# A fused convolution and gated product: row halves of product 2 that share one tile, a moved half-way mark, and new orders for the first four tiles

## The chip, the cores and the metric

The kernel runs on one core of a Trainium2 chip. The metric is the device time of one execution in microseconds, the median of ten runs. Five engines work side by side, each through its own queue in order: TensorE (PE, with its weight loads shown as PEld), VectorE (DVE), ScalarE (ACT), GpSimd (POOL) and SyncE (SP), which here issues nearly all transfers. Engines wait for one another through semaphores.

## The reference, cut to what matters

The input `x` has 8 sequences of 4096 tokens with 192 channels. The first stage is a causal convolution over seven tokens whose weights, one set for each of 8 heads, are a softmax; a head owns 24 channels. The second stage is two matrix products with a gate between them:

```python
w = softmax(weight)                                  # [8, 7]
c = einsum('hk,bskhg->bshg', w, windows_of_7(x))     # causal, zeros ahead of a sequence
h = c.reshape(32768, 192) @ w_in                     # [32768, 2048]
g = h * cos(h)
out = (g @ w_out).astype(float32)                    # [32768, 192]
```

## The kernel before, in words

**Tiles and units.** The 32768 tokens are cut into 64 tiles of 512 (`T`, `NT`) and, for the convolution, into 32 units of 1024 (`U`, `NU`); a unit serves two tiles. The loop over `t` (L409) runs 66 times: in iteration `t` the kernel makes product 1 and the gate for tile `t`, works on product 2 of earlier tiles, and prepares the convolution of unit `t // 2 + 2`, one half of its heads in the even iteration and the other in the odd one.

**A unit's path.** SP loads the unit and its edges (`load_unit`, `load_edges`, L68 to L76), POOL casts it (`cast_unit`, L175), PE convolves it with band matrices (`conv_part`, L214: steps `c1` and `c2`), ACT takes the result out (`ec1`, `ec2`), POOL doubles each row (`double_unit`, L245), SP issues a DMA transpose into `cT` (`turn_unit`, L249), and POOL mends the first tokens of each block of 128 (`mend_edges`, L257). `x_f`, `x_bf`, `ct` and `cT` have two buffers each.

**Product 1 and the gate.** `mm1` (L339) makes one of eight blocks of a tile, `h0` to `h7`: six matmuls of 64 rows by 512 tokens, in pairs that run side by side in the upper and the lower half of the array. A block takes one of three buffers of PSUM, a ring that the convolution's banks also come from. `gcu` (L351), written `s0` to `s7`, takes the sine on ACT and multiplies on DVE, and frees the buffer.

**Product 2.** A step (`mm2_step`, L364) is a pair of 64-row matmuls. There are two banks, `b` = 0 and 1, each for two of a tile's four blocks of 128 tokens. Both row halves of the array have to be summed into each bank[...]. Before the change the upper half works on bank `b` of phase `p`, and the lower half one phase later on the same bank: 129 phases of 32 steps, of which the first and the last have only one half at work. `evac` (L386) copies a finished bank out on ACT, and `store` (L391) sends a tile to memory from SP's queue.

**The turn.** Where the halves change banks, `Turn` (L159 to L170) puts a no-op into SP's queue: the no-op waits for the last matmuls on PE, and the next matmuls on PE wait for the no-op. The convolution does the same between `c1` and `c2`, except in units 0 to 2. In a trace the no-ops are SPq rows of L164.

**Orders.** What each iteration issues on PE is written out in a string: `h3` is a block of product 1, `m12` twelve steps of product 2, `c1` and `c2` the convolution. A second string has the order on ACT and DVE: `s3` is the gate, `P` and `Q` the evacuations of banks 0 and 1. `PE_FIRST` and `ACT_FIRST` are for the first tiles, where `r` is the convolution of unit 0's second half (`conv_rest`, L318) and `d1`, `d2` a further convolution. `p` and `q` in the PE string are only marks: what they release in the program's order is written below the loop over the string (L457 to L478). Since every queue is in order, a mark's place in the string settles where its transfers stand among SP's other entries and its copies among POOL's:

```python
            if k == "q":
                if second == 0 and t and u + 1 < NU:
                    turn_unit(u + 1)
                    mend_edges(u + 1)
                if t == 1:
                    turn_unit(1)
                    cast_unit(3)
                    mend_edges(1)
                if second == 0 and u + 3 < NU:
                    cast_unit(u + 3)
```

**The start.** Unit 0 is loaded, convolved and turned in two parts. Its first half (`conv_first`, `turn_first`) goes through PE for the transpose; its second half is `r`, whose four copies ACT and DVE share, after which POOL doubles it, SP issues its transpose and the loads of unit 2, and POOL casts `w_out`.

Of the kernel before, what the change touches and what calls it, by code (L numbers as in the profile page):

```python
# [8 lines left out]
FP32 = mybir.dt.float32  # L9
# [7 lines left out]
def kernel(  # L17
# [8 lines left out]
    nc = tc.nc  # L26
# [41 lines left out]
    def load_edges(u, queue=nc.sync):  # L68
        queue.dma_start(out=x_tiles[u][:, UB, :],
                          in_=xf[u * U - 8 : u * U - 8 + U, :].rearrange("(n t) d -> n t d", t=128)[:, 0:16, :])  # L70

    def load_unit(u, n0=0, n1=UB, queue=nc.sync):
        if n0 == 0:
            x_tiles[u] = xin.tile([128, UB + 1, D], FP32, name="x_f")
        queue.dma_start(out=x_tiles[u][:, n0:n1, :],
                          in_=xf[u * U + n0 * 128 : u * U + n1 * 128, :].rearrange("(n p) d -> p n d", p=128))  # L76
# [119 lines left out]
    def conv_out(u, c, ps, n0, m0, m1, copy, double=False, banks=(0, 1)):  # L196

        for b in banks:
            w0 = (2 * c + b) * 2 * R
            o = ct_tiles[u][:, m0:m1, :, :, w0 : w0 + 2 * R].rearrange("p n k t w -> p (n k) t w")  # L200
            i = ps[b][:, (m0 - n0) * 2 * G : (m1 - n0) * 2 * G].rearrange("p (m t w) -> p m t w", t=1, w=2 * R)
            if double:
                copy(o, i.to_broadcast([128, (m1 - m0) * NC, 2, 2 * R]))
            else:
                copy(o[:, :, 0, :], i[:, :, 0, :])  # L205

    def ring_banks():
        h = h_pool.tile([128, 2, T], FP32, name="h")
        return [h[:, 0, :], h[:, 1, :]]
# [35 lines left out]
    def double_unit(u, n0=0, n1=UB + 1):  # L245
        ct = ct_tiles[u]
        nc.gpsimd.tensor_copy(out=ct[:, n0:n1, :, 1, :], in_=ct[:, n0:n1, :, 0, :])  # L247

    def turn_unit(u, n0=0, n1=UB + 1):  # L249
        ct = ct_tiles.pop(u)  # L250
        if u not in cT:
            cT[u] = cT_pool.tile([128, UB + 1, NC, 128], BF16, name="cT")
        nc.sync.dma_start_transpose(out=cT[u][:, n0:n1].rearrange("p n c k -> p (n c) k"),
                                    in_=ct[:, n0:n1].rearrange("p n c t k -> p (n c t k)"))
        cT.pop(u - 2, None)
# [62 lines left out]
    def conv_rest():  # L318
        banks = o_banks()
        for c in range(2):  # L320
            for i in range(4):
                for prev in range(2):
                    conv_mm(0, c, [b[:, 4 * G * 2 * c :] for b in banks], i, slice(0, 128), NB + 1 - prev, UB + 1 - prev, prev,
                            start=c == 0 and prev == 0 and i % 2 == 0, stop=c == 1 and prev == 1 and i % 2 == 1)
        for b in range(2):
            for c in range(2):
                conv_out(0, c, [x[:, 4 * G * 2 * c :] for x in banks], NB, NB, UB, copies[1 - b], banks=(b,))

    conv_first()
    turn_first(0)  # L330
# [31 lines left out]
    STEPS = 2 * NF  # L362

    def mm2_step(q):  # L364
        phase, i = divmod(q, STEPS)
        f, si = divmod(i, 2)
        for r in range(2):
            tt, b = divmod(phase - r, 2)
            if not 0 <= tt < NT:
                continue  # L370
            if r == 0 and i == 0:

                last = (tt, b) == (NT - 1, 1)
                o_ps[tt, b] = ring_banks()[0] if last else o_pools[b].tile([128, T], FP32, name="o_ps%d" % b)
            rows = slice(64 * r, 64 * r + 64)
            s = 2 * b + si
            m = nc.tensor.matmul(out=o_ps[tt, b][:, si * D : (si + 1) * D],  # L377
                                 lhsT=g_tiles[tt][rows, f, s * 128 : (s + 1) * 128], rhs=wo[rows, f // 2, f % 2, :],
                                 start=(r == 0 and i == 0), stop=(r == 1 and i == STEPS - 1), skip_group_check=True)
            if r == 0 and i == STEPS - 1:  # L380
                turns[tt, b] = Turn()
                turns[tt, b].mark(m)
            if r == 1 and i == 0:
                turns.pop((tt, b)).wait(m)

    def evac(t, b):  # L386
        if b == 0:
            o_sb[t] = opool.tile([128, NB, D], FP32, name="o_sb")
        nc.scalar.copy(o_sb[t][:, 2 * b : 2 * b + 2, :].rearrange("p s d -> p (s d)"), o_ps.pop((t, b))[:, 0 : 2 * D])  # L389

    def store(t, b0=0, b1=2):  # L391
        nc.sync.dma_start(out=out[t * T + b0 * 256 : t * T + b1 * 256, :].rearrange("(n p) d -> p n d", p=128),
                          in_=o_sb[t][:, 2 * b0 : 2 * b1, :])

    o_ps, o_sb, turns = {}, {}, {}
# [1 line left out]

    PE_ORDER = "h0 m7 c1 m6 c2 m4 h1 m7 q h2 h3 m12 h4 m10 h5 m10 h6 h7 p m8"  # L400
    ACT_ORDER = "s0 ec1 ec2 s1 Q s2 s3 s4 s5 P s6 s7"

    PE_FIRST = ["h0a h0b h1 r h2 h3 h4 d1 d2 h5 h6 c1 c2 h7 p m12",
                "h0 m8 h1 m12 q h2 h3 h4 m4 d1 d2 m8 h5 m8 h6 c1 c2 m8 h7 m4 p m8"]
    ACT_FIRST = ["s0a s0b s1 s2 s3 s4 ed1 ed2 s5 s6 ec1 ec2 s7", "s0 s1 s2 s3 s4 ed1 ed2 s5 s6 ec1 ec2 P s7"]

    HALVES = {"": (0, NB), "a": (0, NB // 2), "b": (NB // 2, NB)}
    step = 0
    for t in range(NT + 2):  # L409
        u, second = divmod(t, TPU)  # L410
        cu, cc = (u + TPU, second) if t >= TPU else (1 + t, 1)
        conv = {"c": conv_part(cu, cc, ring_banks if t else o_banks, t < TPU) if cu < NU else iter(())}
        if t < TPU:
            conv["d"] = conv_part(cu, 0, ring_banks if t else o_banks, True)
        act, done, h = (ACT_ORDER if t > 1 else ACT_FIRST[t]).split(), set(), {}

        def flush():
            while act:
                k = act[0]
                need = {"P": "p", "Q": "q", "e": k[1:2] + "2"}.get(k[0], "h" + k[1:])  # L420
                if need not in done:
                    return
                act.pop(0)
                if k == "P" and 0 <= t - 1 < NT:
                    evac(t - 1, 0)
                elif k == "Q" and 0 <= t - 2 < NT:
                    evac(t - 2, 1)
                elif k[0] == "e":
                    next(conv[k[1]], None)
                elif k[0] == "s" and t < NT:  # L430
                    gcu(t, int(k[1]), h.pop(k[1:]), *HALVES[k[2:]])

        for k in (PE_ORDER if t > 1 else PE_FIRST[t]).split():
            if k[0] == "h" and t < NT:
                h[k[1:]] = mm1(t, int(k[1]), *HALVES[k[2:]])
            elif k[0] in conv:
                next(conv[k[0]], None)
            elif k == "r":
                conv_rest()
                double_unit(0, NB, UB)  # L440
                turn_unit(0, NB, UB)
                load_unit(2)
                load_edges(2)
                for q in range(2):
                    nc.gpsimd.tensor_copy(out=wo[:, q * HP : (q + 1) * HP], in_=wo_f[:, q * HP : (q + 1) * HP])  # L445
            elif k[0] == "m":
                for q in range(step, step + int(k[1:])):
                    mm2_step(q)
                step += int(k[1:])
            elif k[0] == "p":  # L450
                assert step % (2 * STEPS) == 0
            elif k[0] == "q":
                assert step % (2 * STEPS) == STEPS
            done.add(k)
            flush()
# [8 lines that stand above are left out]
                    mend_edges(1)  # L464
                if second == 0 and u + 3 < NU:
                    cast_unit(u + 3)
                if second == 1 and t > 1 and cu < NU:
                    double_unit(cu)
                if t == NT + 1:
                    store(NT - 1, 1, 2)  # L470
            if k == "p":
                if t < NT + 1 and 0 <= t - 2:
                    store(t - 2)
                if t == NT:
                    store(NT - 1, 0, 1)
                if second == 1 and u + 4 < NU:
                    load_unit(u + 4)
                    load_edges(u + 4)  # L478
        if t == 0:
            double_unit(1)  # L480
            load_unit(3)
            load_edges(3)
            cast_unit(2)
        if t == 1:
            double_unit(2)
# [30 lines left out]
```

## Time and profile before

| what | value |
|---|---|
| median of 10 runs | 720.44 us (720.24 to 721.1) |
| the profiled execution | 720.35 us |
| its span, first to last instruction | 718.6 us |
| granted TensorE clock, mean | 0.999 |
| PE busy | 708.1 us (99%) |
| PE weight loads busy | 530.3 us (74%) |
| ACT busy | 617.7 us (86%) |
| DVE busy | 611.4 us (85%) |
| POOL busy | 149.7 us (21%) |
| start of h0 of tiles 1, 2 and 63 | 22.04, 35.48 and 695.98 us |
| DMA transposes on SP's queue | 32, median 4.11 us each |

Times in the timeline count from the first instruction. A row of PE gives the start of its first matmul and the end of its last, so that rows overlap a little; the start of the next row tells when PE was free again. A row on SP's queue (SPq) is the time that the issue of a transfer took there, not the transfer itself. The chain of waits is followed back from the last instruction, and shows which engine's work set the end. Each group of instructions has its busy time, the mean length of one, and the idle time ahead of it with what ended it.

### The profile page before, as it was taken

The page shows a single profiled execution, that of the slowest core. Times are in us where ns is not written, and L with a number is a line of the kernel's source. Part 1 is how long each engine was busy: PE and PEld are TensorE (multiplying, and loading weights), DVE is VectorE, ACT ScalarE, POOL GpSimd, SP SyncE. Part 2 cuts the span into 40 slices and gives each one's busy share as a digit, 9 for nine tenths or more (in the row PEclk, how much of TensorE's full clock was granted, in tenths as well). Part 3 has the DMA queues.
Part 4 walks back from the last instruction along what each step waited for, and adds up shares of the span by engine and source line. Part 5 has one row for each costly group of instructions (what it writes and reads, how often), then busy time and mean ns, then how long its engine had stood idle before and what let it go on. Part 6 is the DMA issues. An engine that isn't in the chain of part 4 may idle for free.

```text
span 718.6 us, 26315 instructions
## 1 busy us (share of the span) xinstructions
PE 708.1 (99%) x11826; PEld 530.3 (74%) x11827; DVE 611.4 (85%) x536; ACT 617.7 (86%) x781; POOL 149.7 (21%) x124
## 2 busy tenths in 40 slices
PE   7899999999999999999999999999999999999997
PEld 3577777777777777777777777777777777777776
DVE  6788888888888888888888888888888888888984
ACT  7888888888888898888888888888888888888884
POOL 5621122221122221022220222220122221121000
PEclk9999999999999999999999999999999999999999
DMA  8745544455534356534455434566434455324312
GB/s 217 181 122 144 137 101 121 86 136 145 125 108 115 88 144 145 113 108 115 100 145 145 117 101 104 114 144 145 109 109 96 123 145 143 103 67 89 80 46 67
DMA packets 183664, 85.24 MB, mean 119 GB/s; under 512 B 111616, under 2 KB 183168, under 8 KB 183552
## 3 DMA queue, kind: packets, MB, share of 16 engines
q1 hardware_dynamic: 183128, 82.78, 46.9%
q8 instruction: 92, 1.51, 0.9%
q0 software_dynamic: 416, 0.79, 0.7%
q14 instruction: 20, 0.16, 0.1%
q10 hardware_dynamic: 8, 0.00, 0.0%
HBM read 31.36 MB, written 25.17 MB: 79 GB/s over the span
## 4 chain that ended last, share of the span: by engine, by line
PE 95%; DMA 2%; POOL 1%; ACT 1%; DVE 0%; issue 0%; SPq 0%; DVEq 0%; POOLq 0%
PE o_ps L377 46%; PE h L347 45%; PE h L190 3%; DMA wo_f<-in_moe_w_out_dram 1%; DMA x_f<-in_x_dram 1%; PE h L377 0%; POOL x_bf L179 0%; POOL wo L445 0%; ACT L148 0%; PE o_ps L292 0%; DVE g L358 0%; DVEq L511 0%; ACT x_bf L179 0%; ACT cs L354 0%; POOL mask L128 0%
## 5 line engine op out<-in xcount | busy, mean ns | idle before, releaser
L358 DVE TENSOR_TENSOR g<-h,cs 128x1024 bf16<-128x1024 f32 (+1 forms) x513 | 603.6, 1218 | 93.8 <-ACT cs L354 89.0
L354 ACT ACTIVATE cs<-h 128x1024 bf16<-128x1024 f32 (+1 forms) x513 | 511.3, 1026 | 59.3 <-PE h L347 52.2
L377 PEld LDWEIGHTS <-g 64*128 64x128 bf16 x8192 | 362.2, 94 | 85.9 <-SPq L164 1.2
L377 PE MATMUL o_ps<-wo,g 64*128 64x192 bf16 x8128 | 423.9, 243 | 1.7 <-ACT o_sb L389 0.6
L347 PE MATMUL h<-cT,w 64*128 64x512 bf16 (+1 forms) x3078 | 398.5, 376 | 0.3 <-DVE cT L316 0.2
L347 PEld LDWEIGHTS <-w 64*128 64x128 bf16 x3078 | 154.7, 94 | 85.3 <-issue 1.1
L259 POOL COPY cT<-cT 128x144 bf16<-128x144 bf16 x31 | 9.5, 307 | 496.1 <-DMA cT<-ct 325.2
L179 POOL CAST x_bf<-x_f 128x1728 bf16<-128x1728 f32 (+1 forms) x32 | 80.5, 2515 | 9.0 <-DMA x_f<-in_x_dram 8.9
L205 ACT CAST ct<-h 128x432 bf16<-128x432 f32 x120 | 56.4, 522 | 27.4 <-PE h L190 26.9
L389 ACT COPY o_sb<-o_ps 128x384 f32<-128x384 f32 x127 | 60.1, 473 | 4.9 <-PE o_ps L377 4.9
L247 POOL COPY ct<-ct 128x1728 bf16<-128x1728 bf16 (+1 forms) x32 | 51.3, 1602 | 18.5 <-ACT ct L205 18.3
L190 PE MATMUL h<-x_bf,band 64*128 64x216 bf16 (+1 forms) x472 | 42.7, 254 | 1.0 <-POOL x_bf L179 1.0
L190 PEld LDWEIGHTS <-band 64*128 64x128 bf16 (+1 forms) x496 | 22.2, 94 | 7.0 <-issue 4.4
L105 PE MATMUL o_ps<-zero 128*128 128x512 bf16 x12 | 5.5, 630 | 1.3 <-DVE zero L100 1.3
L377 PE MATMUL h<-wo,g 64*128 64x192 bf16 x64 | 5.8, 243 | 0.0
L105 PEld LDWEIGHTS <-zero 128*128 128x128 bf16 x15 | 1.7, 129 | 3.5 <-issue 2.2
L190 PE MATMUL o_ps<-x_bf,band 128*128 128x96 bf16 (+1 forms) x24 | 1.9, 223 | 2.4 <-POOL x_bf L179 2.4
L205 ACT CAST ct<-o_ps 128x432 bf16<-128x432 f32 (+1 forms) x6 | 2.4, 461 | 1.0 <-PE o_ps L190 0.9
L445 POOL CAST wo<-wo_f 128x1536 bf16<-128x1536 f32 x2 | 2.9, 1464 | 0.8 <-DMA wo_f<-in_moe_w_out_dram 0.8
L389 ACT COPY o_sb<-h 128x384 f32<-128x384 f32 x1 | 0.5, 478 | 2.4 <-PE h L377 2.4
L115 ACT ACT_TABLE_LOAD x1 | 1.3, 1283 | 1.4 <-PEq L500 1.4
L292 PEld LDWEIGHTS <-band 128*128 128x128 bf16 x32 | 1.1, 96 | 1.2 <-POOL band L279 1.2
(47 smaller groups left out, 27.2 us busy)
## 6 DMA issues: line engine op xcount, KB each, us to landing
out_dram<-o_sb SPq DMA_DIRECT2D x63, 384.0 KB
x_f<-in_x_dram SPq DMA_DIRECT2D x31, 768.0 KB
x_f<-in_x_dram SPq DMA_DIRECT2D x31, 96.0 KB
wo_f<-in_moe_w_out_dram SPq DMA_DIRECT2D x4, 384.0 KB
x_f<-in_x_dram SPq DMA_DIRECT2D x2, 384.0 KB
w<-in_moe_w_in_dram POOLq DMA_DIRECT2D x2, 384.0 KB, 6.3
cT<-ct SPq DMA_TRANSPOSE x32
out_dram<-o_sb SPq DMA_DIRECT2D x2, 192.0 KB
```

The source lines that it names most:

```text
L105: nc.tensor.matmul(out=bank, lhsT=zero[:, 0:128], rhs=zero, start=True, stop=True)
L179: copy(out=bf[u][:, n0 + o : n1 + o, :].rearrange("p n (h k r) -> p (n h) k r", k=NC, r=R), in_=x_tiles[u][:, n0:n1, :].rearrange("p n (h ...
L190: return nc.tensor.matmul(out=ps[i // 2][:, 0 : (n1 - n0) * 2 * G].rearrange("p (n k i r) -> p i n k r", n=n1 - n0, k=NC, i=2)[:, i % 2], ...
L205: copy(o[:, :, 0, :], i[:, :, 0, :])
L247: nc.gpsimd.tensor_copy(out=ct[:, n0:n1, :, 1, :], in_=ct[:, n0:n1, :, 0, :])
L259: nc.gpsimd.tensor_copy(out=cT[u][:, 0:UB, :, 0 : K - 1], in_=cT[u][:, UB].rearrange("p c (n t) -> p n c t", t=16)[:, :, :, 8 : 8 + K - 1])
L347: nc.tensor.matmul(out=h[:, i, n0 * 128 : n1 * 128], lhsT=w[rows, k, j, :], rhs=c[rows, m0 + n0 : m0 + n1, k, :], start=(k == 0), stop=(k ...
L354: nc.scalar.activation(out=cs[:, :, part], in_=h[:, :, part], func=AF.Sin, bias=math.pi / 2.0, scale=1.0)
L358: nc.vector.tensor_tensor(out=g_tiles[t][:, 2 * j : 2 * j + 2, part], in0=h[:, :, part], in1=cs[:, :, part], op=ALU.mult)
L377: m = nc.tensor.matmul(out=o_ps[tt, b][:, si * D : (si + 1) * D], lhsT=g_tiles[tt][rows, f, s * 128 : (s + 1) * 128], rhs=wo[rows, f // 2, ...
L389: nc.scalar.copy(o_sb[t][:, 2 * b : 2 * b + 2, :].rearrange("p s d -> p (s d)"), o_ps.pop((t, b))[:, 0 : 2 * D])
L445: nc.gpsimd.tensor_copy(out=wo[:, q * HP : (q + 1) * HP], in_=wo_f[:, q * HP : (q + 1) * HP])
```

## The change

*Product 2.* A tile now has 64 steps in one run. In its first 32 the upper row half sums bank 0 and the lower one bank 1; in the other 32 they have changed places. One turn for each tile, in its middle, holds both matmuls of a pair. Both banks of a tile are finished together.

*Evacuation and stores.* Both banks are evacuated behind the mark `p`: bank 0 by ACT, bank 1 by DVE. The last tile has both banks in the ring, and its two halves are stored from SP's and from ACT's queue.

*Marks.* `p` now stands where a tile is finished, behind `h2`, and `q` where it is half done, behind `h6`; before they stood at the end of the string and behind `h1`. The doubling of a unit, the store of a tile and the loads go with `p` (the loads of iteration 1 with `q`); the transpose, the mending and the cast stay with `q`.

*The start.* Four tiles have orders of their own. `r` comes two blocks later. Its copies become an entry `er` of the ACT order, write each row twice, and POOL's doubling of that half goes; the transpose, the loads of unit 2 and the casts of `w_out` are issued with `er`.

```diff
@@ conv_rest
+        yield
         for b in range(2):
             for c in range(2):
-                conv_out(0, c, [x[:, 4 * G * 2 * c :] for x in banks], NB, NB, UB, copies[1 - b], banks=(b,))
+                conv_out(0, c, [x[:, 4 * G * 2 * c :] for x in banks], NB, NB, UB, copies[1 - b], True, (b,))
+        yield
@@ mm2_step
-        phase, i = divmod(q, STEPS)
-        f, si = divmod(i, 2)
+        tt, i = divmod(q, 2 * STEPS)
+        half, k = divmod(i, STEPS)
+        f, si = divmod(k, 2)
...
         for r in range(2):
-            tt, b = divmod(phase - r, 2)
...
+            b = half ^ r
             rows = slice(64 * r, 64 * r + 64)
             s = 2 * b + si
...
+        if i == STEPS - 1:
+            turns[tt] = Turn()
+            turns[tt].mark(*ms)
+        if i == STEPS:
+            turns.pop(tt).wait(*ms)
@@ evac, store
-        nc.scalar.copy(o_sb[t][:, 2 * b : 2 * b + 2, :].rearrange("p s d -> p (s d)"), o_ps.pop((t, b))[:, 0 : 2 * D])
+        copies[b](o_sb[t][:, 2 * b : 2 * b + 2, :].rearrange("p s d -> p (s d)"), o_ps.pop((t, b))[:, 0 : 2 * D])
...
@@ orders
-    PE_ORDER = "h0 m7 c1 m6 c2 m4 h1 m7 q h2 h3 m12 h4 m10 h5 m10 h6 h7 p m8"
-    ACT_ORDER = "s0 ec1 ec2 s1 Q s2 s3 s4 s5 P s6 s7"
+    PE_ORDER = "h0 m1 c1 m6 c2 m4 h1 m10 h2 p h3 m10 h4 m9 h5 m9 h6 m4 q h7 m11"
+    ACT_ORDER = "s0 ec1 ec2 Q s1 P s2 s3 s4 s5 s6 s7"
-    PE_FIRST = ["h0a h0b h1 r h2 h3 h4 d1 d2 h5 h6 c1 c2 h7 p m12",
-                "h0 m8 h1 m12 q h2 h3 h4 m4 d1 d2 m8 h5 m8 h6 c1 c2 m8 h7 m4 p m8"]
-    ACT_FIRST = ["s0a s0b s1 s2 s3 s4 ed1 ed2 s5 s6 ec1 ec2 s7", "s0 s1 s2 s3 s4 ed1 ed2 s5 s6 ec1 ec2 P s7"]
+    PE_FIRST = ["h0a h0b h1 h2 h3 r h4 h5 d1 d2 h6 c1 c2 h7",
+                "p h0 m2 h1 m7 h2 m8 h3 m1 h4 m2 h5 m12 q d1 d2 m4 h6 m6 c1 c2 m2 h7 m8",
+                "h0 m1 c1 m6 c2 m2 h1 m3 p h2 h3 m8 h4 m12 h5 m10 h6 m2 q h7 m6",
+                "h0 m7 c1 m6 c2 m5 h1 m8 p h2 h3 m12 h4 m5 h5 m8 h6 m7 q h7 m11"]
+    ACT_FIRST = ["s0a s0b s1 s2 er s3 s4 s5 ed1 ed2 s6 ec1 s7 ec2", "s0 s1 s2 s3 s4 s5 ed1 ed2 s6 ec1 ec2 s7",
+                 ACT_ORDER, "s0 ec1 Q ec2 s1 P s2 s3 s4 s5 s6 s7"]
@@ flush: what er releases
+                    if k == "er":
+                        turn_unit(0, NB, UB)
+                        load_unit(2)
+                        load_edges(2)
+                        for q in range(2):
+                            nc.gpsimd.tensor_copy(out=wo[:, q * HP : (q + 1) * HP], in_=wo_f[:, q * HP : (q + 1) * HP])
@@ marks
+            if k == "p":
                 if second == 1 and t > 1 and cu < NU:
                     double_unit(cu)
+                if 0 <= t - 2 < NT - 1:
+                    store(t - 2)
                 if t == NT + 1:
                     store(NT - 1, 1, 2)
...
+                    store(NT - 1, 0, 1, nc.scalar)
+            if k == ("p" if t > 1 else "q") and second == 1 and u + 4 < NU:
+                load_unit(u + 4)
+                load_edges(u + 4)
```

More of the change, by code (lines that the diff above doesn't have):

```diff
@@ L364, in mm2_step @@
     def mm2_step(q):
-        phase, i = divmod(q, STEPS)
-        f, si = divmod(i, 2)
-        for r in range(2):
-            tt, b = divmod(phase - r, 2)
[L369 to L374, printed above, removed]
+        tt, i = divmod(q, 2 * STEPS)
+        half, k = divmod(i, STEPS)
+        f, si = divmod(k, 2)
@@ L375, in mm2_step @@
+        if tt >= NT:
+            return
+        if i == 0:
+            for b in range(2):
+                o_ps[tt, b] = (ring_banks()[0] if tt == NT - 1 else
+                               o_pools[b].tile([128, T], FP32, name="o_ps%d" % b))
+        ms = []
+        for r in range(2):
+            b = half ^ r
             rows = slice(64 * r, 64 * r + 64)
             s = 2 * b + si
-            m = nc.tensor.matmul(out=o_ps[tt, b][:, si * D : (si + 1) * D],
-                                 lhsT=g_tiles[tt][rows, f, s * 128 : (s + 1) * 128], rhs=wo[rows, f // 2, f % 2, :],
-                                 start=(r == 0 and i == 0), stop=(r == 1 and i == STEPS - 1), skip_group_check=True)
@@ L380, in mm2_step @@
[L380 to L384, printed above, removed]
+            ms.append(nc.tensor.matmul(out=o_ps[tt, b][:, si * D : (si + 1) * D],
+                                       lhsT=g_tiles[tt][rows, f, s * 128 : (s + 1) * 128], rhs=wo[rows, f // 2, f % 2, :],
+                                       start=(i == 0), stop=(i == 2 * STEPS - 1), skip_group_check=True))
@@ L386, in evac @@
+        if i == STEPS - 1:
[3 more added lines that the diff above has]
+            turns.pop(tt).wait(*ms)
     def evac(t, b):
-        if b == 0:
+        if t not in o_sb:
             o_sb[t] = opool.tile([128, NB, D], FP32, name="o_sb")
-        nc.scalar.copy(o_sb[t][:, 2 * b : 2 * b + 2, :].rearrange("p s d -> p (s d)"), o_ps.pop((t, b))[:, 0 : 2 * D])
-    def store(t, b0=0, b1=2):
-        nc.sync.dma_start(out=out[t * T + b0 * 256 : t * T + b1 * 256, :].rearrange("(n p) d -> p n d", p=128),
+        copies[b](o_sb[t][:, 2 * b : 2 * b + 2, :].rearrange("p s d -> p (s d)"), o_ps.pop((t, b))[:, 0 : 2 * D])
@@ L393, in store @@
+    def store(t, b0=0, b1=2, queue=nc.sync):
+        queue.dma_start(out=out[t * T + b0 * 256 : t * T + b1 * 256, :].rearrange("(n p) d -> p n d", p=128),
                           in_=o_sb[t][:, 2 * b0 : 2 * b1, :])
     o_ps, o_sb, turns = {}, {}, {}
-    PE_ORDER = "h0 m7 c1 m6 c2 m4 h1 m7 q h2 h3 m12 h4 m10 h5 m10 h6 h7 p m8"
-    ACT_ORDER = "s0 ec1 ec2 s1 Q s2 s3 s4 s5 P s6 s7"
-    PE_FIRST = ["h0a h0b h1 r h2 h3 h4 d1 d2 h5 h6 c1 c2 h7 p m12",
-                "h0 m8 h1 m12 q h2 h3 h4 m4 d1 d2 m8 h5 m8 h6 c1 c2 m8 h7 m4 p m8"]
@@ L414 @@
             conv["d"] = conv_part(cu, 0, ring_banks if t else o_banks, True)
-        act, done, h = (ACT_ORDER if t > 1 else ACT_FIRST[t]).split(), set(), {}
+        if t == 0:
+            conv["r"] = conv_rest()
+        act, done, h = (ACT_ORDER if t >= len(ACT_FIRST) else ACT_FIRST[t]).split(), set(), {}
         def flush():
@@ L419, in flush @@
                 k = act[0]
-                need = {"P": "p", "Q": "q", "e": k[1:2] + "2"}.get(k[0], "h" + k[1:])
+                need = {"P": "p", "Q": "p", "e": "r" if k == "er" else k[1:2] + "2"}.get(k[0], "h" + k[1:])
                 if need not in done:
@@ L423, in flush @@
                 act.pop(0)
[L424 to L427, printed above, removed]
+                if k[0] in "PQ":
+                    if 0 <= t - 2 < NT:
+                        evac(t - 2, "PQ".index(k[0]))
                 elif k[0] == "e":
                     next(conv[k[1]], None)
+                    if k == "er":
[4 more added lines that the diff above has]
+                            nc.gpsimd.tensor_copy(out=wo[:, q * HP : (q + 1) * HP], in_=wo_f[:, q * HP : (q + 1) * HP])
                 elif k[0] == "s" and t < NT:
                     gcu(t, int(k[1]), h.pop(k[1:]), *HALVES[k[2:]])
-        for k in (PE_ORDER if t > 1 else PE_FIRST[t]).split():
+        for k in (PE_ORDER if t >= len(PE_FIRST) else PE_FIRST[t]).split():
             if k[0] == "h" and t < NT:
@@ L437 @@
                 next(conv[k[0]], None)
[L438 to L445, printed above, removed]
             elif k[0] == "m":
@@ L466 @@
                     cast_unit(u + 3)
+            if k == "p":
                 if second == 1 and t > 1 and cu < NU:
                     double_unit(cu)
+                if 0 <= t - 2 < NT - 1:
+                    store(t - 2)
                 if t == NT + 1:
                     store(NT - 1, 1, 2)
[L471 to L478, printed above, removed]
+                    store(NT - 1, 0, 1, nc.scalar)
+            if k == ("p" if t > 1 else "q") and second == 1 and u + 4 < NU:
+                load_unit(u + 4)
+                load_edges(u + 4)
         if t == 0:
```

## The prediction

> **What bounds the kernel now.** I read the page's engine totals and chain first, then the timeline of one steady tile, then the same for SP's queue, then SP's waits.
>
> ```profile
> PE 708.1 (99%) x11826; PEld 530.3 (74%) x11827; DVE 611.4 (85%) x536; ACT 617.7 (86%) x781; POOL 149.7 (21%) x124
> ...
> PE 95%; DMA 2%; POOL 1%; ACT 1%; DVE 0%; issue 0%; SPq 0%; DVEq 0%; POOLq 0%
> ...
> L358 DVE TENSOR_TENSOR g<-h,cs 128x1024 bf16<-128x1024 f32 (+1 forms) x513 | 603.6, 1218 | 93.8 <-ACT cs L354 89.0
> L354 ACT ACTIVATE cs<-h 128x1024 bf16<-128x1024 f32 (+1 forms) x513 | 511.3, 1026 | 59.3 <-PE h L347 52.2
> ...
> L389 ACT COPY o_sb<-o_ps 128x384 f32<-128x384 f32 x127 | 60.1, 473 | 4.9 <-PE o_ps L377 4.9
> ```
>
> The chain is PE's own stream: work added on ACT or DVE is free while it fits, but a PE wait after the start is lost outright. The timeline (start, length, engine and line):
>
> ```profile
> 342.86 1.46 PE L347 MATMUL h<-cT,w 64*128 64x512 bf16 x12
> 343.21 4.10 SPq L253 DMA_TRANSPOSE cT<-ct  x1
> ...
> 344.16 1.15 PE L377 MATMUL o_ps<-wo,g 64*128 64x192 bf16 x24
> 345.15 0.81 PE L347 MATMUL h<-cT,w 64*128 64x512 bf16 x6
> ...
> 348.42 0.38 SPq L392 DMA_DIRECT2D out_dram<-o_sb  x1
> ...
> 350.05 0.81 PE L347 MATMUL h<-cT,w 64*128 64x512 bf16 x6
> 350.69 0.74 PE L377 MATMUL o_ps<-wo,g 64*128 64x192 bf16 x14
> 351.28 0.36 PE L190 MATMUL h<-x_bf,band 64*128 64x216 bf16 x4
> 351.46 0.67 PE L377 MATMUL o_ps<-wo,g 64*128 64x192 bf16 x12
> 351.95 0.36 PE L190 MATMUL h<-x_bf,band 64*128 64x216 bf16 x4
> ```
>
> Prices from start to start: two h take 344.16-342.86 = 1.30, so one h 0.65; twelve steps 0.99, so a step 0.0825; half a conv 0.18. A tile is 8 x 0.65 + 64 x 0.0825 + 0.36 = 10.85 us. The row halves of conv and of product 2 change banks through a no-op on SP (L164): it waits for the matmuls, then PE waits for it. The transpose is issued on the same queue. SP's timeline in the head, and its waits (total, times, longest):
>
> ```profile
> 18.17 1.53 SPq L253 DMA_TRANSPOSE cT<-ct  x1
> 19.75 0.90 SPq L75 DMA_DIRECT2D x_f<-in_x_dram  x1
> ```
>
> ```profile
> SPq L164 <- PE o_ps L377: 351.1, 127, 5.2
> SPq L164 <- PE h L190: 126.4, 58, 2.9
> ```
>
> The load starts 0.05 us after the transpose's row ends (19.70): SP does nothing beside it. In the steady tiles SP's no-ops wait for PE, never for SP: after `q` the transpose ends at 347.31 and the next no-op is due at 348.3 (its row's start), 1.0 us later. The old order leaves exactly that hole.
>
> [...] the trace's 128x384 DVE copy (L316) took 0.56, so I take 0.56.
>
> **The change, part by part.**
>
> *Product 2 without its half-filled ends.* Steps fall from 129 x 32 to 128 x 32: 32 x 0.0825 = 2.64 us less PE work. By the end of tile 3 the new orders have done 171 steps against 200, 29 fewer; the last three are in the tail.
>
> *Evacuations.* Bank 1 leaves ACT for DVE: ACT loses 64 x 0.47 = 30 us, DVE gains 64 x 0.56 = 36 us. DVE in a tile: 8 x 1.16 (back to back, 4.78 for four gives 1.2 with the tail) + 0.56 = 9.8 to 10.3 of 10.85. Walked through a tile from its h0: the half ends behind m10 at 3.39; Q on DVE 3.56 to 4.1; product 1 on DVE to 5.3; h4, which needs that ring slot, starts at 5.51. h3 ends at 4.69 and P (ACT) is done by 4.3. So nothing waits, with 0.2 us to spare: cost 0, up to 0.2 a tile if DVE's copy is slower.
>
> *The turn in mid-tile* has one h (0.65) over it, not two. Round trip without cover: last matmul 711.99, next weights 712.25, so 0.26 with its own 0.08 slot. Covered; cost 0.
>
> *Where `q` went.* turn_unit(u+1) still hangs on `q`, and `q` moves from behind h1 (3.64 us into the tile: 350.05 to 353.69) to behind h6: 7 x 0.65 + 53 x 0.0825 + 0.36 = 9.27. Queued on SP behind the transpose then stands the conv no-op of the next tile. Counted from h7's start B: the transpose starts at B+0.35 (343.21-342.86), takes 4.11 (median of its row), and SP is free at B+4.46. The no-op and PE's answer cost some 0.15 (0.05 row gap, 0.1 of the round trip), so c2 can start at B+4.61. PE reaches c2 at h7 0.65 + m11 0.91 + h0 0.65 + m1 0.08 + c1 0.18 + m6 0.49 = B+2.96. PE stands 1.65 us. All of PE queues behind it, and ec1, ec2, s1 behind PE; nothing makes it up, because PE has no idle time. It happens in each odd tile that has a conv behind a transposing tile: 3, 5 ... 59, 29 times. 28 x 1.65 + 1.55 (tile 3, whose order has six more steps before c1, five fewer after h7) = 47.8 us. Ends: the shortest steady transposes (4.06) give 1.6 each, the longest (4.84) 2.4; if SP were not held, 0.
>
> *Moved with `p`.* double_unit (POOL, 1.63), load_unit and load_edges (0.50 and 0.81 of SP) go to behind h2, five h's ahead of the next mark, after a store of 0.38: SP is busy some 1.8 of 5 us. Hidden. cT lands 6 to 8 us after its issue (61.15 to POOL's L259 at 67.2; 25.43 to 33.73), mend adds 0.31; from B it is needed at 1.56 + 10.85 + 1.65 = 14. Hidden.
>
> *The head.* conv_rest behind h3: 16 matmuls, 0.82, same price. Its four copies, doubled, go behind s2 on ACT (two, 0.48 each) and behind the product of h2 on DVE (two, 0.56); POOL's copy of 0.82 goes. The transpose is issued near 16.8 instead of 18.17, after w_out's last issue, and unit 2's loads follow 1.4 earlier; the casts of w_out keep their transfers' times. ACT has 8 sines and six copies in tile 0 and frees the o banks near 22.6. Tile 1 then needs 5 h and 32 steps to `q`, 5.9 and some 0.3 of ring waits: 28.8, where before the transpose row began at 25.43. So the transpose of unit 1 goes out at 29.1 and, landing 6 to 8.3 later and mended, lets tile 2 start at 35.6 to 37.8; I take 36.1. PE would be there at 32.9: a wait of 3.2 takes the gain of the fewer steps. Before, tile 2 began at 35.48. Tiles 2 and 3: 9.67 of PE work and some 0.5 waiting for ACT after the stop, then 11.4: tile 4 at 57.7 against 35.48 + 2 x 10.85 = 57.2. Head: +0.5 (-0.5 to +2).
>
> *The tail.* From h0 of tile 63: before 718.6 - 695.98 = 22.6. After: 8.91 to h7, 0.65, 96 steps 7.92, one bare turn 0.18, latency and the longer copy 0.75, then 3.1 to 3.4 for the store as before (715.58 to 718.6), two halves at once: 21.6. -1.0.
>
> Sum: 47.8 + 0.5 - 1.0 = +47.3 on the span of 718.6, 765.9. The profiled execution took 720.35, 1.75 over its span, and the median is 720.44: 765.9 + 1.8 = 767.7.
>
> **Rivals.** *SP is not held.* If the no-op can pass while the transpose's row runs, or the row shortens below 2.45 us (2.96 - 0.35 - 0.15, the point from which no stall is left), only head and tail remain: -0.5, so 719.9, no change; with tile 2 unstopped it would be 717. For it: no steady no-op of before ever stood behind a transpose, so the trace shows the hold only for a load. Against: 19.75 after 19.70. *DVE becomes the bound.* If Q and product 1 end 0.2 us later than walked, h4 waits in each tile not already relieved by the stall, 30 x 0.2 = 6: 774 with the stalls, 726 without. Against: 10.3 of 10.85. *The transpose is slower where it now runs*, over the next tile's start: at 4.6 each stall is 2.1, 29 x 2.1 = 61, giving 781. Against: x loads are now 16 us old by then, and the store waits behind it.
>
> **How the numbers follow.** The stall as sized: 0.78. SP not held: 0.11, of which 0.05 faster. DVE late, with stalls: 0.06. Longer transposes: 0.05. The likeliest gives 768. Its ends are 29 stalls of 1.4 to 1.9 and the head's -1 to +1.5: 759 to 777, which takes in the DVE case. I leave out the unheld case and the longest transposes. A difference of 0.2% (1.4 us) is about what a measurement can tell from none. Faster 0.05, same 0.06, slower 0.89.
>
> **What would show it.** Right: PEld of L190 waiting for SPq L164 29 times, 1.6 us each; L164 rows starting 0.05 after a transpose's end; odd tiles 12.5 long, even ones 10.85; PE h L347 waiting near 33 us for the mended cT; 64 DVE copies at 0.56. Wrong: L164 rows inside a transpose's row, or PE at 99% again. What I know least is whether a no-op is held as a load is.

## The result, and the profile after

The changed kernel takes 774.92 us (median of 8 runs, 774.3 to 778.85) against 720.45 us (29 runs, 720.18 to 721.1): a recorded ratio of 1.0763 (the two medians alone give 1.0756), 95% interval 1.0754 to 1.0773. It is 54.5 us slower. The profiled execution took 774.3 us, with a span of 772.6.

From the page of the changed kernel, its engine totals and the chain that ended last:

```profile
span 772.6 us, 26315 instructions
...
PE 713.2 (92%) x11826; PEld 516.2 (67%) x11827; DVE 647.1 (84%) x600; ACT 602.9 (78%) x717; POOL 147.9 (19%) x123
...
PE 78%; SPq 17%; issue 2%; ACT 1%; DMA 1%; POOL 1%; DVE 0%; POOLq 0%
PE h L349 37%; PE o_ps L382 37%; SPq L253 16%; PE h L190 3%; DMA x_f<-in_x_dram 1%; PE h L382 1%; ACT cs L356 0%; POOL x_bf L179 0%; DVE g L360 0%; ACT L148 0%; ACT x_bf L179 0%; SPq L164 0%; POOL mask L128 0%; SPq L75 0%; PE o_ps L292 0%
...
L394 DVE COPY o_sb<-o_ps 128x384 f32<-128x384 f32 x63 | 35.1, 557 | 82.2 <-PE o_ps L382 81.8
...
L394 ACT COPY o_sb<-o_ps 128x384 f32<-128x384 f32 x63 | 29.9, 474 | 2.6 <-PE o_ps L382 2.6
```

Before, 95% of the chain was PE and SP had none of it. Now the issue of transposes, L253 on SP's queue, holds 16% of the path to the end. The chain counts each transpose's row whole, 29 x 4.29 = 124 us; how much of that PE stood still is read below. PE's work has hardly grown, but its share of the span has fallen by seven points.

The waits of the changed kernel say how that issue reaches PE (engine and line, what it waited for, total, times, longest):

```profile
PEld L190 <- SPq L164: 53.5, 29, 2.4
...
PE h L190 <- SPq L164: 46.9, 29, 2.2
...
PE h L349 <- POOL cT L259: 2.5, 1, 2.5
```

The weight loads and the matmuls of the convolution's second half (`c2`) waited 29 times for a no-op on SP, where there were no such waits. An odd tile in the timeline of the changed kernel:

```profile
351.74 0.81 PE L349 MATMUL h<-cT,w 64*128 64x512 bf16 x6
352.08 4.10 SPq L253 DMA_TRANSPOSE cT<-ct  x1
...
354.03 0.35 PE L190 MATMUL h<-x_bf,band 64*128 64x216 bf16 x4
...
354.21 0.66 PE L382 MATMUL o_ps<-wo,g 64*128 64x192 bf16 x12
...
356.28 0.12 PEld L190 LDWEIGHTS <-band 64*128 64x128 bf16 x4 [1.64 <-SPq L164]
356.29 0.36 PE L190 MATMUL h<-x_bf,band 64*128 64x216 bf16 x4 [1.41 <-SPq L164]
```

The transpose's row ends at 356.18, and `c2` starts 0.11 us later. It was due when the six steps ahead of it (12 matmuls) had started, at 354.21 + 6 x 0.0825 = 354.70, so PE lost 1.59 us. This tile's h0 starts at 353.30 and the next at 365.72: 12.42 us. The even tile ahead of it took 10.83, so that a pair lasts 23.25 where it took 21.69.

Something that was not forecast stands in the timeline at 590:

```profile
590.32 0.36 PE L190 MATMUL h<-x_bf,band 64*128 64x216 bf16 x4 [2.01 <-SPq L164]
590.52 0.62 PE L382 MATMUL o_ps<-wo,g 64*128 64x192 bf16 x8
590.93 1.49 PE L349 MATMUL h<-cT,w 64*128 64x512 bf16 x6
592.21 1.81 PE L382 MATMUL o_ps<-wo,g 64*128 64x192 bf16 x20
593.81 1.64 PE L349 MATMUL h<-cT,w 64*128 64x512 bf16 x12
595.28 0.99 PE L382 MATMUL o_ps<-wo,g 64*128 64x192 bf16 x20
```

Behind a wait of over 2 us, one h takes 1.28 us from start to start instead of 0.65, and ten steps 1.60 instead of 0.83: for 3.41 us the granted clock, the share of TensorE's full speed, is one half (0.50 over 590.75 to 594.15). The trace's clock records have two such spells before the end, at 143.6 and 590.8. In each PE gets through 1.7 us of work less than at full speed, so the two cost 3.4 us.

The span adds up. The gaps before `c2` beyond the normal step, from the starts of the matmuls, sum to 52.1 us over 29 tiles; the two spells are 3.4. 772.6 - 718.6 = 54.0, so everything else together gained 1.5 us: some 0.4 in the tail, and about 1 in the steady tiles, where a pair without its wait takes 23.25 - 1.59 = 21.66 instead of 21.69.

### The profile page after: what moved, and what is told of

It reads as the page before. It is cut to its first block, busy times and chain, and to the rows that moved or that the text cites. A ratio compares the mean times of both kernels' runs of the same rounds, so it can differ in the third digit from the quotient of the medians.

```text
span 772.6 us, 26315 instructions
## 1 busy us (share of the span) xinstructions
PE 713.2 (92%) x11826; PEld 516.2 (67%) x11827; DVE 647.1 (84%) x600; ACT 602.9 (78%) x717; POOL 147.9 (19%) x123
## 4 chain that ended last, share of the span: by engine, by line
PE 78%; SPq 17%; issue 2%; ACT 1%; DMA 1%; POOL 1%; DVE 0%; POOLq 0%
PE h L349 37%; PE o_ps L382 37%; SPq L253 16%; PE h L190 3%; DMA x_f<-in_x_dram 1%; PE h L382 1%; ACT cs L356 0%; POOL x_bf L179 0%; DVE g L360 0%; ACT L148 0%; ACT x_bf L179 0%; SPq L164 0%; POOL mask L128 0%; SPq L75 0%; PE o_ps L292 0%
## 5 line engine op out<-in xcount | busy, mean ns | idle before, releaser
L382 PEld LDWEIGHTS <-g 64*128 64x128 bf16 x8192 | 354.9, 94 | 98.9 <-issue 1.5
L349 PE MATMUL h<-cT,w 64*128 64x512 bf16 (+1 forms) x3078 | 406.9, 377 | 5.3 <-POOL cT L259 2.5
L349 PEld LDWEIGHTS <-w 64*128 64x128 bf16 x3078 | 144.3, 94 | 83.7 <-issue 4.1
L394 DVE COPY o_sb<-o_ps 128x384 f32<-128x384 f32 x63 | 35.1, 557 | 82.2 <-PE o_ps L382 81.8
L247 POOL COPY ct<-ct 128x1728 bf16<-128x1728 bf16 x31 | 50.4, 1627 | 0.1
L394 ACT COPY o_sb<-o_ps 128x384 f32<-128x384 f32 x63 | 29.9, 474 | 2.6 <-PE o_ps L382 2.6
```

What stands on the lines that cost most here:

```text
L349: nc.tensor.matmul(out=h[:, i, n0 * 128 : n1 * 128], lhsT=w[rows, k, j, :], rhs=c[rows, m0 + n0 : m0 + n1, k, :], start=(k == 0), stop=(k ...
L382: ms.append(nc.tensor.matmul(out=o_ps[tt, b][:, si * D : (si + 1) * D], lhsT=g_tiles[tt][rows, f, s * 128 : (s + 1) * 128], rhs=wo[rows, f ...
L394: copies[b](o_sb[t][:, 2 * b : 2 * b + 2, :].rearrange("p s d -> p (s d)"), o_ps.pop((t, b))[:, 0 : 2 * D])
```

## The experiments

My theory was the forecast's: the no-op between `c1` and `c2` stands behind the transpose in SP's queue, and PE waits. The rivals were that product 2 in its new form or the DVE copies cost something in each tile, or that the transfer itself does the harm. Below, "the half-way no-op" is the turn of product 2 in the middle of a tile.

**One move undone.** The transpose goes back to a place early in its tile; all else stays as changed.

```diff
@@ q
-                    turn_unit(u + 1)
                     mend_edges(u + 1)
@@ p
                     store(t - 2)
+                if second == 0 and t and u + 1 < NU:
+                    turn_unit(u + 1)
```

> The changed kernel with one move: in even tiles the transpose of the next unit is queued on SP behind p's store instead of behind q; mending and cast stay at q. Theory (the conv no-op stands behind the transpose's 4.1 us on SP): the transpose now ends some 0.1 to 0.6 us before the half-way no-op is due, so the 29 waits of 52.1 us in all go, and the two spells of halved clock (3.4 us lost) with them: span 772.6 - 55.5 = 717.1, time about 719. Rival (product 2 in one run, or the evacuation on DVE, costs something in each tile): the time stays over 730. Rival (head and tail alone gain as their 2.6 us fewer steps say): 716.

Measured: 723.76 us, ratio 1.0045 (1.0031 to 1.0059). 51 of the 54.5 us are gone, with all 29 waits of the convolution and both clock spells. It stays 5 us above the number expected. SP's rows around one half-way mark, and the weight load that waits there, show why:

```profile
83.37 0.38 SPq L397 DMA_DIRECT2D out_dram<-o_sb  x1
...
83.85 5.61 SPq L253 DMA_TRANSPOSE cT<-ct  x1
...
89.56 0.86 PEld L382 LDWEIGHTS <-g 64*128 64x128 bf16 x22 [0.81 <-SPq L164]
```

Right behind a store the transpose's row is longer. The line view of this experiment's transposes, and that of the changed kernel, in that order (shortest, median, longest in ns):

```profile
L253 SPq DMA_TRANSPOSE cT<-ct x32: 2516/4837/5818, 16.8 to 672.5; - x32
```

```profile
L253 SPq DMA_TRANSPOSE cT<-ct x32: 2396/4119/4838, 16.8 to 728.2; - x32
```

With 4.84 in place of 4.12 the margin ahead of the half-way no-op is gone, and PE waited for SP 15 times there, 8.7 us by its weight loads. Its tiles lost less: tiles 4 to 62 take 641.95 us, 4.1 more than in the later experiment without these waits. The wait that was removed had come back in small at another no-op.

**The no-op removed instead, the transposes left late.**

```diff
-conv_part(cu, cc, ring_banks if t else o_banks, t < TPU)
+conv_part(cu, cc, ring_banks if t else o_banks, True)
```

> The changed kernel with the transposes left where they are, and every convolution made as the first units' are: four matmuls over all 128 rows, one after the other, with no change of banks and so no no-op between c1 and c2. Theory (the no-op carries the wait): no PE wait behind SP is left although SP is held as before; the convolution costs 0.12 to 0.3 us more in each of 60 tiles (0.48 against 0.36 in the first tiles[...]), so 719 + 7 to 18 = 726 to 737. Rival (the transpose or its transfer slows PE by itself, or cT comes late): 765 or more.

Measured: 732.28 us (two runs, 731.72 and 732.84). The convolution without a change of banks, with the transpose on SP right across it:

```profile
355.71 4.07 SPq L253 DMA_TRANSPOSE cT<-ct  x1
...
357.59 0.25 PE L382 MATMUL o_ps<-wo,g 64*128 64x192 bf16 x2
357.77 0.54 PE L190 MATMUL h<-x_bf,band 128*128 128x216 bf16 x4
358.25 1.00 PE L382 MATMUL o_ps<-wo,g 64*128 64x192 bf16 x20
```

From the end of the step (357.67) to the next steps it takes 0.58 us against 0.36, 0.10 of it ahead of its first matmul. That is 0.22 more, 13 us over 58 tiles (I had expected 60, but tiles 0 and 1 had no such no-op before and tiles 60 to 63 have no convolution). The profiled execution also has one clock spell in the head; the other run, at a granted clock of 0.999, has a span of 730.0: the 717.2 of a later experiment, which has no waits for SP, and the 13. No wait for SP is left at the convolution. So the transposes that run beside PE here cost nothing that shows (730.0 - 717.2 = 12.8, against the 13 of the convolution); it was the no-op behind them that cost. The 0.12 to 0.3 expected had its lower end from the first tiles, 0.48 against 0.36; its upper end was my estimate. No run keeps the row halves and leaves the no-op out, so whether they need it is not shown.

**The same move alone, in the kernel before.** The transpose and the mending move from `q` to `p`, behind the store.

```diff
@@ q
-                if second == 0 and t and u + 1 < NU:
-                    turn_unit(u + 1)
-                    mend_edges(u + 1)
@@ p
+                if second == 0 and t and u + 1 < NU:
+                    turn_unit(u + 1)
+                    mend_edges(u + 1)
```

> The kernel before with one move: in even tiles the transpose and the mending go from q to p, behind the store. Theory: SP begins the transpose at once behind the store, at 348.85 on the clock of the profile of before, and is free at 353.0; c2, due at 351.95, starts near 353.1. That is 1.1 us for the median transpose and up to 1.9 for the longest, 1.3 on average, 29 times: 720.4 + 37 = 757. Rival (the stalls need the new product 2 or the DVE copies): 720 to 722.

Measured: 785.57 us (784.21 and 786.94). Direction, place and count are as expected, the size is not: 65 us instead of 37.

```profile
402.01 0.38 SPq L392 DMA_DIRECT2D out_dram<-o_sb  x1
402.52 4.76 SPq L253 DMA_TRANSPOSE cT<-ct  x1
...
407.38 0.11 PEld L190 LDWEIGHTS <-band 64*128 64x128 bf16 x4 [1.85 <-SPq L164]
```

The transposes stand behind a store here too, and take 4.80 in the median instead of the 4.11 I had priced, some 20 us in 29. The 29 gaps, less a normal step each, sum to 60 us, and there are four clock spells (6.8 us). None of the new product 2, the DVE copies or the new orders is in this kernel, so the harm needs only the order of two entries in SP's queue.

**The suspected cost doubled.** Each late transpose is issued twice, the first time into a spare tile.

```diff
+    spare = consts.tile([128, UB + 1, NC, 128], BF16)
...
                 if second == 0 and t and u + 1 < NU:
+                    ct = ct_tiles[u + 1]
+                    nc.sync.dma_start_transpose(out=spare.rearrange("p n c k -> p (n c) k"),
+                                                in_=ct.rearrange("p n c t k -> p (n c t k)"))
                     turn_unit(u + 1)
```

> The changed kernel with each transpose of the even tiles issued twice, the first time into a spare tile that nobody reads. Theory: SP is held 4.2 us longer and each of the 29 waits grows by that: 774.9 + 29 x 4.2 = 897. If a PE idle of some 6 us also halves the clock for 3.4 us each time, as two idles of 2.2 us did in the changed kernel, 1.7 us are added 29 times: 946. Rival (the wait is for the transfer's landing, or something else): under 800.

Measured: 967.86 us, one run. From its waits:

```profile
PEld L190 <- SPq L164: 179.7, 29, 6.7
```

6.2 us in place of 1.8, 29 times: 126 us more against the 122 expected. The rest is the clock, whose mean is 0.904. Its records show half speed for 184 us before the end, in spells of 3.41 or 6.83 us: one with each of these waits and one in the head. 39 of the 184 us fall into the waits themselves, where PE had nothing to do; the other 145 cost half, 73. I had counted one spell of 3.41 for each wait, 49 us; 24 of the 29 are 6.83 long. 774.9 - 3.4 (the two spells already in it) + 126 + 73 = 970, against 968 measured.

**The transpose ahead of the store.** As the first experiment, with the two entries of `p` exchanged.

```diff
+                if second == 0 and t and u + 1 < NU:
+                    turn_unit(u + 1)
                 if 0 <= t - 2 < NT - 1:
                     store(t - 2)
```

> As e1_turn_at_p, but with the transpose queued ahead of p's store instead of behind it. In e1 the transposes took 4.8 us and up to 5.8 behind a store that SP had issued 0.05 us earlier, against 4.1 elsewhere, and ten half-way no-ops came 0.3 to 0.9 us late. Theory (what is left in e1 over 719 is the longer row behind a store): here SP reaches the transpose right after the conv no-op, 1.2 us into the tile, its rows are 4.1 again, no half-way no-op is late, and the time is 718.9, which is head and tail alone: 717.5 to 719.5. Rival (the row is long wherever it runs beside c2 and h1): as e1, 723.

Measured: 720.04 us (21 runs, 718.54 to 720.95), ratio 0.9987 (0.9981 to 0.9994). The profiled execution took 718.94 and its span is 717.2, against 717.1 worked out from the changed kernel. No half-way no-op is late.

The spread of 2.4 us goes with the clock. One spell of 3.41 us at half speed takes 1.7 / 717, or 0.002, off a run's mean. The ten runs with a mean granted clock of 0.999 or more took 718.5 to 719.4, the eleven at 0.997 or 0.998 took 720.0 to 721.0. So, by this estimate, the 718.9 expected holds for the runs without a half-clock spell, and the median stands among those with one. The spell probably lies in the head, behind PE's wait of 2.5 us for the mended `cT` of unit 1: the experiment with the whole convolution has one at 37.3, behind the same wait, which ends there at 35.8, and the next experiment, which takes this wait away, has no run below 0.999. The trace of this kernel has no spell (mean clock 1.000), so its place is not shown.

Its transposes have a median of 4.14 us, but several in a row at 4.5 to 4.9 remain, without a store ahead of them. So a row has two reasons to be longer. A store right ahead of it adds some 0.7 us. The other comes back about every eight transposes, in the kernel before as well: there at 104.6 and 126.3, 278.1 and 299.8, 451.7 and 473.4, and 646.9; here from 145 to 210, 340 to 383 and 513 to 578. In the first experiment the two add up to rows of 5.1 to 5.8. What sets this rhythm stays open.

**Unit 1's transpose early as well.** This experiment and the two after it start from the kernel just measured, with the transpose ahead of the store; only what is new is shown.

```diff
@@ q
                 if t == 1:
-                    turn_unit(1)
                     cast_unit(3)
@@ p
+                if t == 1:
+                    turn_unit(1)
```

> e5_turn_before_store with unit 1's transpose moved from q to p of iteration 1, the first mark there; cast and mending stay at q. Theory (the 2.5 us wait of tile 2's h0 for the mended cT eats the gain of 32 steps less): SP issues it near 24.4 as soon as POOL has doubled unit 1, it lands by 32.6, h0 of tile 2 waits 0 to 0.5 us instead of 2.5: 718.9 - 2.3 = 716.6. Rival (tile 2 is then held by ACT or by the casts instead): 718 or more.

Measured: 716.24 us (715.95 to 716.77), ratio 0.9941 (0.9927 to 0.9955) to the kernel before: faster than both by 4.3 and 58.7 us. In its timeline unit 1's transpose goes out at 23.70, `cT` is mended before PE asks for it, and tile 2 starts at 32.97 instead of 35.72 (in the changed kernel):

```profile
23.70 5.25 SPq L253 DMA_TRANSPOSE cT<-ct  x1
...
32.48 0.31 POOL L259 COPY cT<-cT 128x144 bf16<-128x144 bf16 x1 [1.89 <-DMA cT<-ct]
...
32.97 0.81 PE L349 MATMUL h<-cT,w 64*128 64x512 bf16 x6
```

**Unit 0's copies not doubled.**

```diff
-                conv_out(0, c, [x[:, 4 * G * 2 * c :] for x in banks], NB, NB, UB, copies[1 - b], True, (b,))
+                conv_out(0, c, [x[:, 4 * G * 2 * c :] for x in banks], NB, NB, UB, copies[1 - b], banks=(b,))
@@ er
+                        double_unit(0, NB, UB)
                         turn_unit(0, NB, UB)
```

> e5_turn_before_store with unit 0's second half copied once and doubled by POOL, as in the kernel before, in the place of er. Theory: POOL doubles it at 17.4 to 18.2 behind unit 1's cast, the transpose starts near 18.3 instead of 16.8, h0 of tile 1 starts 0.5 us later, and unit 2's loads 1.4 later, which the cast hides: 0.3 to 1 us over e5. Rival (the doubling in the copies is what the head needs): 2 us or more over e5.

Measured: 719.91 us (12 runs, 719.22 to 721.96), ratio to before 0.9995 (0.9987 to 1.0003), against 720.04 with the doubling. These medians can't be compared as they stand, because both kernels have runs at a mean clock of 0.999 or more and runs at 0.995 to 0.998. Of the runs at a granted clock of 0.999 or more, the six here have a median of 719.36 (719.22 to 719.46), the ten with the doubling 718.87 (718.54 to 719.39). So this part of the change gains some 0.5 us, within the 0.3 to 1 expected. The profiles agree: without it tile 1 starts at 22.12 instead of 21.77 and tile 2 at 36.04 instead of 35.67, and the spans are 717.6 and 717.2.

**Both evacuations on ACT.**

```diff
-        copies[b](o_sb[t][:, 2 * b : 2 * b + 2, :].rearrange("p s d -> p (s d)"), o_ps.pop((t, b))[:, 0 : 2 * D])
+        nc.scalar.copy(o_sb[t][:, 2 * b : 2 * b + 2, :].rearrange("p s d -> p (s d)"), o_ps.pop((t, b))[:, 0 : 2 * D])
```

> e5_turn_before_store with both evacuations on ACT, as in the kernel before. It says how much stands behind the DVE copy. Q takes ACT at 3.56 to 4.0 of a tile, in front of s1, so s1 ends at 5.0, P at 5.45, and the step behind h3, due at 4.69, waits 0.8 us; h4 waits for the product of h1. Some 0.8 in each of 62 tiles: 718.9 + 50 = 769. Rival (ACT has the time, it is busy 78%): 719 to 722.

Measured: 768.93 us (768.21 and 769.64). The steps behind h3 wait in 61 tiles; from the timeline of this kernel, `h2` and `h3` on PE and what follows, and ACT's queue meanwhile (Q, then the sine of `s1`, then P):

```profile
354.52 1.48 PE L349 MATMUL h<-cT,w 64*128 64x512 bf16 x12
354.71 0.48 ACT L394 COPY o_sb<-o_ps 128x384 f32<-128x384 f32 x1 [0.84 <-PE o_ps L382]
355.09 1.03 ACT L356 ACTIVATE cs<-h 128x1024 bf16<-128x1024 f32 x1
...
356.01 0.48 ACT L394 COPY o_sb<-o_ps 128x384 f32<-128x384 f32 x1
...
356.54 1.00 PE L382 MATMUL o_ps<-wo,g 64*128 64x192 bf16 x20 [0.55 <-ACT o_sb L394]
```

Two h fill 1.30, so PE was free at 355.82 and stood until 356.54: 0.72 us, in 61 tiles 44 of the 49 us over the transpose-ahead kernel. ACT is busy for 80% of this kernel's span. Q, in front of `s1`, keeps ACT idle for 0.84 us until product 2 has ended; the sine and P follow late, and the steps behind `h3` need the bank that P empties. So what costs here is where Q stands in its queue, not how busy ACT is. Q on ACT at another place of the order was not tried.

## Why the prediction was right, and where its terms were off

The forecast was 768 (759 to 777), slower; measured 774.92. By its own steps:

*The place of `q`* was right: which entry stands behind which, the tiles concerned (29), and the wait of a typical tile, 1.59 us measured against 1.65 forecast. What was mis-sized is the sum. I multiplied by the median transpose (4.11); ten of the 29 waits are 1.95 to 2.35 us, behind transposes of 4.4 to 4.8, so the sum is 52.1 instead of 47.8. The profile of before already had such rows (its longest is 4.84), and I used them for the range only. A sum needs the mean: it is 4.23 over 29 rows of before, and would have given 51.3.

*The clock.* The forecast held that a PE wait costs its own length. Two spells of half clock, of 3.41 us each, added 3.4 us here. They stood behind two of ten waits of 1.95 to 2.35 us, the shorter of them 2.2, and in the third experiment four stood behind 29 waits of 1.7 to 2.8 us. So in this kernel a wait of 2.2 us is not safe, though eight of the ten of that size passed without a spell; what decides between them is not shown. Other runs of the changed kernel have a mean granted clock between 0.988 and 0.996, and the slowest run (778.85) has the lowest, so much of their spread is probably the number of such spells. That 774.92 lies in the range is in part luck: no term stood for the clock, and its 3.4 us took room that the range kept for longer stalls and for the head (up to +1.5). The 774 of the second rival comes near the measured time by chance.

*The head.* Forecast +0.5 to the start of tile 4, before tile 3's wait; measured 59.30 - 2.11 = 57.19 against 57.15, nothing. The wait of tile 2 for the mended `cT` is 2.5 us (3.2 forecast), and the move of unit 1's transpose alone gave it back (2.7 us between the spans of the two profiles, 717.2 and 714.5).

*The tail.* Forecast -1.0; measured from h0 of tile 63 22.23 us against 22.65, so -0.4. The last copies end when I had said, 8.91 + 9.5 after that h0; the two stores at once then take 3.7 us to the end of the span instead of 3.1 to 3.4.

*Costs set at nothing.* DVE's copy takes 557 ns (560 assumed) and even tiles stay at 10.83 us. The half-way turn under one h waits for nothing while SP is free (PE's only wait for SP there is 0.33 us, at the bare turn of the tail), and the loads at `p` hold up nobody. The first rival, that SP is free beside the row, is shown false: in the changed kernel every transpose is followed by SP's next entry within 0.06 us of its end. The second, DVE too late, did not occur. The third, slower transposes where they now run, hardly occurred: 29 rows have a mean of 4.29 us against 4.23 before, 1.8 us in all. So of the 6.7 us that the span lies above the forecast sum, 4.3 are waits, most of it the median used for the mean; 3.4 are the clock; head and tail took 0.1 more than forecast, and the steady tiles gave back about 1.

## What to carry to other kernels

A queue that carries both transfers and signals between steps of another engine is priced by the time its longest issue holds it (here 4.1 to 4.8 us for a transpose, 0.38 for a store). When you move a transfer, look for the next signal behind it and ask when its waiter is due. Balance engines by where an instruction stands in its queue, not by busy share: one copy of 0.47 us in front of the wrong sine, in each tile, cost 49 us, and one transpose of 4.1 us in front of the wrong no-op, in every second tile, cost 54. When the waits of a dense PE stream pass some 2 us, allow for half-clock spells on top: here 6 of 19 waits of 1.95 to 2.8 us had one behind them, at 1.7 us each. Compare runs of such a kernel with an eye on their granted clock, because one spell can be larger than the effect looked for (1.7 us, where the doubled copies made 0.5).

## What the runs showed of the hardware that was not expected

- A transpose of 27 blocks issued some 0.1 us behind a store holds SP for 4.80 to 4.84 us in the median, against 4.12 elsewhere, and up to 5.8. Apart from that, rows of 4.4 to 4.9 us come back about every eight transposes.
- In the odd tiles of two profiles (the changed kernel and the third experiment) half-clock spells of 3.41 us followed 6 of the 19 PE waits of 1.95 to 2.8 us and none of the 39 shorter ones, of 1.5 to 1.95; they came with every one of the 29 waits of about 6 us behind the doubled transposes, 24 of them 6.83 long.
- Two stores of 192 KB on SP's and ACT's queue at once ended 3.7 us after the copies; one store of that size had taken 3.1 in the kernel before.
